# T in runs spread by ScalarE, the next Gram turn among the last rows, three edits in the last four chunks

## The chip, the cores and the metric

One core of a Trainium2 chip runs the whole program. The metric is the device time of one execution in microseconds (us). The kernel before was timed three times: 463.32, 463.43 and 470.28 us, median 463.43 us.

## The reference

Two blocks follow each other. The first is a delta-rule attention over 4 batches, 8 heads, 768 steps and head dimension 48; the second sends each of the 3072 tokens through one of 8 experts, chosen by a hash of its id.

```python
k_n = k / (np.linalg.norm(k, axis=-1, keepdims=True) + 1e-06)
for t in range(S):
    y[:, :, t] = einsum('bhd,bhde->bhe', q[:, :, t], state)
    v_old = einsum('bhde,bhd->bhe', state, k_n[:, :, t])
    state = state + beta_t * einsum('bhd,bhe->bhde', k_n[:, :, t], v[:, :, t] - v_old)
# x = y as (3072, 384)
for e in range(8):
    xe = x[expert == e]
    out[expert == e] = relu(xe @ w1[e]) @ w2[e]      # w1 384 x 1024, w2 1024 x 384
```

## The kernel before, in words

**Chunks and groups.** The 768 steps are cut into 24 chunks of 32 steps, and four chunks make a group, so there are six groups, 0 to 5. All batches and heads run together: 4 batches by 32 steps fill the 128 partitions. Within a chunk the recurrence is solved with the inverse T of a unit triangular matrix of 32 by 32 for each head and batch.

**The inverse (`inverse(g)`, VectorE).** For the four chunks of group g at once, a transpose of 32x32 blocks turns the Gram matrices (copied out of PSUM by ScalarE, L505) into NT, so that each partition holds one matrix (L628, "the Gram turn"). Then the norms follow: ssq (L630), a square root on ScalarE (root, L633), a short chain of small VectorE instructions (L635 to L649), and Ni (L652). Then 31 rows, each of a product (tmp, L664), a row (U, L660) and an addition (U, L668), each needing the one before. At the end one transpose takes U back to TU (L682), written with steps: one column of each block stands 32 elements from the next.

**The spread (`spread_t(g)`).** The matmul that applies T reads Tz, in which T stands twice, each time with half of the partitions set to zero. For group 0 and for the chunks 1 to 3 of each group this is done by four DMAs from TU (L592), issued by GpSimd and for the last group by SyncE; for the first chunk of groups 1 to 5 by two VectorE products with the columns of kmask (L584).

**A chunk (`chunk(c)`).** TensorE asks the state with the keys (L701 into bank A, on top of V scaled by VectorE in `scale_v`, L605); ScalarE copies the result to R (L733); TensorE asks with the queries into bank Y (L701); it multiplies R with Tz ("the T product", L743 bank<-R,Tz or solo<-R,Tz); ScalarE copies to W (L764); TensorE makes the Gram matrix of chunk c+9 (L485, while there is one) and the update of the state (L774); ScalarE copies the new state to S (L853), in the last four chunks VectorE copies half (L851); TensorE finishes the output with W and MT (L743 bank<-W,MT) and turns K and Q of chunk c+10 (L451). ScalarE copies the output to x_sb (L799), the turned keys to KQ (L461) and two masked copies to MT (L574); VectorE masks the Gram matrix of q and k (GQ, L508). GpSimd scatters x_sb to x_scratch in DRAM (`store`, L805). From chunk SOLO = 15 there is no Gram matrix left to make, and `scale_v`, the first ask, R, the T product and W go in two halves of four heads, the second half in a bank of its own (`home_a`).

**What sets the order.** Every step is a `task` with an engine, a duration that its author gave it, names that it reads and writes, and a boost. `order()` plays these tasks in time and picks on each engine the ready task with the longest rest; the instructions are then emitted in that order, so on every engine the order is fixed when the program is built, and an instruction that has to wait holds up all behind it on its engine.

**After the chunks.** `seven_first` (L112) multiplies the first 288 rows of expert 0 with w1; `turned` (L1472) then with w2. The first w1 and w2 are loaded in seven parts by GpSimd (`first_parts`, L180 and L183; the profile calls both homes w_first), after the stores of the chunks that PARTS lists. The other experts follow, bound to the same core.

Of the kernel before, what the change touches and what calls it, by code (L numbers as in the profile page):

```python
# [13 lines left out]
ACT = mybir.ActivationFunctionType  # L14
ALU = mybir.AluOpType
# [5 lines left out]
def kernel(  # L21
# [24 lines left out]
    QN = P // TB  # L46
# [141 lines left out]
    SP = mybir.EngineType.SP  # L188
# [12 lines left out]
    with ExitStack() as phase1:  # L201
        NU = S // C
        GC = 4
        NG = NU // GC
# [2 lines left out]
        L = C // 2  # L207
        NX = GC * H
        LEAD, AHEAD = 9, 10
        SPLIT, SOLO = NU - GC, NU - LEAD  # L210

        st = phase1.enter_context(tc.tile_pool(name="st", bufs=1))
# [5 lines left out]
        def quarter(b):  # L218
            return slice(C * b, C * b + C)
# [21 lines left out]
        TUs = tiles(2, "TU", [P, NX, C])  # L241
# [23 lines left out]
        kmask = st.tile([P, 2], F32)  # L265
# [15 lines left out]
        def task(eng, ns, reads, writes, emit, kb=0, kind=None, more=0, boost=0, apart=False,  # L281
                 size=0, shy=0):
            writes = tuple(writes) + tuple(x for w in writes for x in cleared.pop(w, ()))
            deps = {writer[r] for r in reads if r in writer}
            for r in reads:
                if r in BANKS and not apart:
                    deps |= {j for j in readers.get(r, ()) if tasks[j]["eng"] != eng}
            for w in writes:
                deps |= readers.get(w, set())
                if w in writer:  # L290
                    deps.add(writer[w])
            i = len(tasks)
# [12 lines left out]
            for w in writes:  # L305
                writer[w] = i
                readers[w] = set()
            return i
# [93 lines left out]
        def four(name):  # L402
            return tuple(f"{name}{b}" for b in range(B))
# [62 lines left out]
        hheads = (range(0, HU), range(HU, H))  # L466
# [109 lines left out]

        def spread_t(g):
            Tz, TU = Tzs[g % 2], TUs[g % 2]
            near = 1
            for cc in range(near if g else 0):  # L580
                xs_ = slice(H * cc, H * cc + H)
                for e in range(2):
                    task("DVE", 270, (f"TU{g % 2}",), (f"Tz{g % 2}{cc}{e}", f"Tz{g % 2}{cc}{e}+"),
                         lambda e=e, xs_=xs_: nc.vector.tensor_scalar(  # L584
                             out=Tz[:, xs_, e], in0=TU[:, xs_], scalar1=kmask[:, e:e + 1],
                             scalar2=None, op0=ALU.mult), boost=5e4)
            for b in range(B if near < GC else 0):
                x0 = H * near
                last = g == NG - 1
                task("SP" if last else "POOL", 450 if last else 800, (f"TU{g % 2}",),  # L590
                     [f"Tz{g % 2}{cc}{b % 2}" + "+" * (b // 2) for cc in range(near, GC)],
                     lambda b=b, x0=x0, eng=nc.sync if last else nc.gpsimd: eng.dma_start(  # L592
                         out=Tz[quarter(b), x0:, b % 2], in_=TU[quarter(b), x0:]),
                     kb=40 if last else 150)

        def scale_v(c):
            g = c // GC
            n = n_toks[g % 3][:, H * (c % GC):H * (c % GC) + H]
            if c == SOLO:
                late["solo"] = len(tasks) + 1  # L600
            for i, hs in enumerate(hheads if c >= SOLO else (range(H),)):
                m = len(hs)
                task("DVE", 482 if c < SOLO else 300, four(f"v{c % 4}_") + (f"ntok{g % 3}",),
                     ("A",) if i == 0 else ("P0", "P1", "P") if c == SOLO else ("P1",),
                     lambda i=i, hs=hs, m=m: nc.vector.tensor_tensor(  # L605
                         home_a(i)[:, 0:m * D].rearrange("p (h d) -> p h d", h=m),
                         Vs[c % 4][:, hs.start:hs.stop],
                         n[:, hs.start:hs.stop, None].to_broadcast([P, m, D]), op=ALU.mult),
                     shy=700 if c else 0)
# [4 lines left out]
        def inverse(g):  # L614
            i = g % 2
            U, Ni, n_tok = Us[i], Nis[i], n_toks[g % 3]
            ssq, root, rn, nd = [smalls[n][i] for n in ("ssq", "root", "rn", "nd")]

            def dve(ns, reads, writes, emit):
# [4 lines left out]
                U, zero[:, :, None].to_broadcast([P, C, C]), ACT.Copy), shy=24000 if g == 1 else 8000 if g else 0, boost=-6e4 if g else 0)  # L624
            task("DVE", 1165, tuple(f"GK{g % 3}{cc}{r}{b}" for cc in range(GC) for r in range(2)
                                     for b in (range(B) if g == 0 and cc < 2 else ("",))) + (
                f"U{1 - i}r{C - 1}",),
                 ("NT",), lambda: nc.vector.transpose(  # L628
                     NT, GKs[g % 3].rearrange("p j c u r -> p j (c u r)")))
            task("DVE", 100, ("NT",), (f"ssq{i}",), lambda: nc.vector.tensor_scalar(  # L630
                out=ssq, in0=NT.rearrange("p j i -> p (j i)")[:, ::C + 1], scalar1=1e-30,
                scalar2=None, op0=ALU.max))
# [4 lines left out]
                out=rn, in0=rn, scalar=0.25, in1=ssq, op0=ALU.mult, op1=ALU.mult))  # L637
            dve(105, ("root", "rn"), ("root",), lambda: nc.vector.scalar_tensor_tensor(
                out=root, in0=rn, scalar=1e-6, in1=root, op0=ALU.add, op1=ALU.add))
# [5 lines left out]
                     out=nd, in0=rn, scalar=-1.0, in1=beta_i[:, g], op0=ALU.mult, op1=ALU.mult))  # L645
# [24 lines left out]
            for j in range(C - 1):  # L670
                n, row = j + 1, f"Ni{i}_{0 if j < L else L}"
                rows = [f"U{i}r{x}" for x in range(C)]
# [6 lines left out]
                if n < C - 1:  # L679
                    task("DVE", ns, (f"U{i}", f"tmp{2 * i + j % 2}"), rows[n + 1:],  # L680
                         lambda j=j: ahead(j, "add"), kind="inv0" if g == 0 else "inv")
            task("DVE", 1810, (f"U{i}", *rows), (f"TU{g % 2}",), lambda: nc.vector.transpose(  # L682
                TUs[g % 2].rearrange("p x i -> p i x"), U))
            last_iv[0] = len(tasks) - 1

        last_iv, first = [0], {}
# [5 lines left out]

        def ask(c, a, bank, name):
            S0, KQ = Ss[c % 2], KQs[c % NKQ]
            apart = c >= SOLO and a == 0

            def go(us):
                res = home_a(us.start) if apart else bank
                x0 = us.start if apart else 0
                for u, b in pairs(us):  # L700
                    nc.tensor.matmul(res[quarter(b), 2 * D * (u - x0):2 * D * (u - x0 + 1)],  # L701
                                     lhsT=KQ[:, u, a, quarter(b)],
                                     rhs=S0[:, b, u].rearrange("p r d -> p (r d)"),
                                     start=(a == 1 and u == 0), stop=True,
                                     skip_group_check=True, tile_position=(0, C * b))

            for us in halves:
                task("PE", 345, held(c, a) + (f"S{c % 2}0", f"S{c % 2}1"),
                     ("P1",) if apart and us.start else (name,),
                     lambda us=us: go(us), kind="A", size=32)  # L710

        def chunk(c):
            g, cc = divmod(c, GC)
            R, W, x_sb = Rs[c % 2], Ws[c % 2], Xs[c % 2]
            TU, Tz, MT = TUs[g % 2], Tzs[g % 2], MTs[c % 2]
            x0 = H * cc
            flat_a, flat_y = bank_a[:, 0:H * D], bank_y[:, 0:H * D]
            turned, grams = next(to_turn, None), next(to_gram, None)
            busy = grams is not None
# [7 lines left out]

            if c > 0:
                ask(c, 0, bank_a, "A")
            for i, hs in enumerate((range(H),) if busy else hheads):  # L730
                task("ACT", 425 if busy else 300, ("P1" if i else "A",),
                     [f"R{c % 2}{x}" for x in range(2) if hheads[x].start in hs],
                     lambda i=i, hs=hs: nc.scalar.activation(  # L733
                         R[:, hs.start:hs.stop].rearrange("p h d -> p (h d)"),
                         home_a(i)[:, 0:D * len(hs)], ACT.Copy))
# [25 lines left out]
            for i, hs in enumerate((range(H),) if busy else hheads):  # L761
# [4 lines left out]
                         scale=-1.0))  # L766
            if busy:
                gram(grams, home="P")()
            if c < NU - 1:
# [14 lines left out]
                for r in range(2):  # L784
# [3 lines left out]
                         apart=True)  # L788
# [8 lines left out]
            if busy and grams % GC == GC - 1:  # L797
                inverse(grams // GC)
            task("ACT", 387, ("Y",), (f"x{c % 2}",), lambda: nc.scalar.activation(  # L799
                x_sb[:, :, 0:DQ].rearrange("p q (i r) -> p q i r", i=CO),  # L800
                flat_y.rearrange("p (q r i) -> p q i r", q=QN, i=CO), ACT.Copy, scale=-1.0))

            def store():
                nc.gpsimd.tensor_copy(x_sb[:, :, DQ], number[:, c])
# [30 lines left out]
                    task("POOL", 900, reads, names, lambda n=n: w_parts(regs[3], first.get(  # L835
                        "w2"))[n](nc.gpsimd), kb=512 if n < CO else 384)

        PARTS = (13, 14, 16, 19, 20, 21, 21)
        to_load = {w: iter(range(AHEAD + 1, NU)) for w in "kq"}
        to_turn, to_gram = iter(range(AHEAD, NU)), iter(range(LEAD, NU))  # L840

# [353 lines left out]
        with tc.manual_schedule():  # L1195
# [13 lines left out]
            for i, bits in enumerate((C - 1, C)):  # L1209
                nc.vector.tensor_scalar(out=low_i[:, i:i + 1], in0=row_i, scalar1=bits,  # L1210
                                        scalar2=None, op0=ALU.bitwise_and)
# [42 lines left out]
    with tc.tile_pool(name="w_pool2", bufs=2) as w_pool2, \  # L1254
# [248 lines left out]
        with tc.manual_schedule():  # L1503
# [25 lines left out]
            hs = {0: m_h.tile([P, FO, CAP], F32, name="h_sb")}  # L1529
# [35 lines left out]
            e = E - 2  # L1565
# [73 lines left out]
```

## Time and profile before

| what | before |
|---|---|
| median of three runs | 463.43 us |
| the profiled execution | 466.5 us |
| its span on the core | 464.9 us |
| TensorE busy | 424.5 us, 91% |
| VectorE busy | 372.6 us, 80% |
| ScalarE busy | 206.6 us, 44% |
| GpSimd busy | 180.2 us, 39% |
| mean granted TensorE clock | 0.957 |

The profile is of one execution. Its times are counted from the start of its span. A row of the view in order of time gives start, duration, engine, line, operation, the tile written and the tiles read, and in brackets the idle time of the engine before it with what ended it. Neighbouring instructions of one kind are merged into a row with their count. The duration of a short instruction overlaps with the next one's start, so what an instruction costs its engine is the distance to the next start.

### The profile page before, as it was taken

How to read it: one execution, taken by the hardware profiler on the slowest of the kernel's cores; microseconds unless marked ns; L12 is line 12 of the kernel's file. 1: busy time of each engine (PE TensorE's matmuls, PEld its weight loads, DVE VectorE, ACT ScalarE, POOL GpSimd, SP SyncE). 2: the span in 40 equal slices, each digit the busy share in tenths (PEclk: the TensorE clock that was granted, in tenths of full speed). 3: DMA queues.
4: the chain of work that ended last, by engine and by line, in shares of the span. 5: the costliest groups of instructions: out<-in, count | busy, mean ns of one | idle time of the engine just before them, and what ended most of it. 6: DMA issues, size and time to landing. Idle time of an engine off the chain costs nothing. (4 is left out here: it accounts for less than half of the span.)

```text
span 464.9 us, 17367 instructions
## 1 busy us (share of the span) xinstructions
PE 424.5 (91%) x7032; PEld 385.9 (83%) x7032; DVE 372.6 (80%) x1229; ACT 206.6 (44%) x477; POOL 180.2 (39%) x228
## 2 busy tenths in 40 slices
PE   6878888988987988789999999999999999999994
PEld 3765777877876877678999998998999999999983
DVE  6799899999899899988638888676977878746750
ACT  3568967776766677645342322031131221300220
POOL 9490412314113234224006250075371653707762
PEclk8588899999898899989999999999999999999998
DMA  7984645657557167344199990190651924101101
GB/s 139 136 158 104 111 96 110 126 107 131 98 109 123 42 147 188 94 89 131 64 256 327 327 312 30 43 310 28 178 192 19 287 76 146 38 5 33 34 31 49
DMA packets 100625, 58.38 MB, mean 126 GB/s; under 512 B 87254, under 2 KB 94945, under 8 KB 99648
## 3 DMA queue, kind: packets, MB, share of 16 engines
q1 hardware_dynamic: 91440, 40.06, 37.0%
q0 software_dynamic: 7824, 16.87, 13.2%
q8 instruction: 56, 0.92, 0.9%
q10 hardware_dynamic: 1280, 0.32, 0.4%
q14 instruction: 25, 0.20, 0.2%
HBM read 44.51 MB, written 10.65 MB: 119 GB/s over the span
## 5 line engine op out<-in xcount | busy, mean ns | idle before, releaser
L1480 POOL DMA_INDIRECT out_dram<-o_sb,idx x81 | 87.5, 1080 | 104.0 <-DVE part L101 59.0
L805 POOL DMA_INDIRECT x_scratch<-x_sb,slot x24 | 25.6, 1066 | 108.2 <-ACT x_sb L799 35.1
L664 DVE TENSOR_TENSOR tmp<-U,Ni 128x30 f32<-128x30 f32 (+9 forms) x180 | 57.9, 322 | 0.1
L668 DVE TENSOR_TENSOR U<-U,tmp 128x30 f32<-128x30 f32 (+9 forms) x180 | 57.9, 322 | 0.0
L701 PE MATMUL bank<-S,KQ 128*32 128x96 f32 x1328 | 36.6, 258 | 6.4 <-ACT S L853 5.4
L660 DVE SCALAR_TENSOR_TENSOR U<-U,Ni 128x1 f32<-128x1 f32 (+30 forms) x186 | 42.2, 227 | 0.3
L853 ACT ACTIVATE S<-psS 48x768 f32<-48x768 f32 x43 | 34.6, 805 | 17.3 <-PE psS L774 16.8
L701 PEld LDWEIGHTS bank<-S,KQ 128*32 128x32 f32 x1328 | 30.0, 115 | 11.0 <-ACT S L853 8.1
L112 PE MATMUL first<-xT,w_sb 128*128 128x190 f32 (+3 forms) x150 | 32.8, 327 | 0.0
L774 PE MATMUL psS<-W,K 32*112 32x96 f32 x736 | 27.3, 276 | 4.4 <-issue 3.1
L743 PE MATMUL bank<-W,MT 64*64 64x48 f32 x768 | 29.5, 226 | 1.8 <-issue 1.7
L164 ACT ACTIVATE h_sb<-h_sb 128x392 f32<-128x392 f32 (+3 forms) x28 | 14.7, 525 | 36.2 <-DVE h_sb L101 36.2
L101 DVE TENSOR_TENSOR h_sb<-part,first 128x196 f32<-128x196 f32 (+3 forms) x63 | 20.3, 352 | 12.5 <-PE first L112 11.7
L743 PEld LDWEIGHTS bank<-W,MT 64*64 64x64 f32 x768 | 26.1, 140 | 4.6 <-issue 2.4
L774 PEld LDWEIGHTS psS<-W,K 32*112 32x112 f32 x736 | 22.6, 177 | 7.7 <-issue 3.8
L112 PE MATMUL first<-h_sb,w_sb 128*128 128x380 f32 (+4 forms) x96 | 27.7, 442 | 0.0
L101 DVE TENSOR_TENSOR part<-part,first 128x196 f32<-128x196 f32 (+4 forms) x50 | 17.5, 349 | 11.9 <-PE first L112 5.0
L112 PEld LDWEIGHTS first<-xT,w_sb 128*128 128x128 f32 x150 | 25.9, 190 | 0.0
L416 POOL DMA_DIRECT2D Q<-in_q_dram x40 | 23.1, 585 | 6.9 <-PE early L451 6.6
L112 PEld LDWEIGHTS first<-h_sb,w_sb 128*128 128x128 f32 x96 | 21.8, 254 | 4.8
L592 POOL DMA_DIRECT2D Tz<-TU x20 | 14.6, 738 | 26.6 <-ACT R L733 12.4
L112 PE MATMUL first<-x_sum,w_sum 128*128 128x196 f32 (+3 forms) x126 | 24.0, 326 | 0.0
(292 smaller groups left out, 1031.4 us busy)
## 6 DMA issues: line engine op xcount, KB each, us to landing
w_sb<-in_moe_w_dram SPq DMA_DIRECT2D x10, 1536.0 KB
w_first<-in_moe_w_dram SPq DMA_DIRECT2D x4, 1536.0 KB
V<-in_v_dram SPq DMA_DIRECT2D x96, 48.0 KB
K<-in_k_dram SPq DMA_DIRECT2D x89, 48.0 KB
Q<-in_q_dram SPq DMA_DIRECT2D x56, 48.0 KB
xr<-x_scratch SPq DMA_DIRECT2D x16, 145.5 KB
Q<-in_q_dram POOLq DMA_DIRECT2D x40, 48.0 KB, 3.7
Tz<-TU POOLq DMA_DIRECT2D x20, 96.0 KB
```

What stands on the lines that cost most here:

```text
L101: return lambda: nc.vector.tensor_tensor(out, a, b, op=ALU.add)
L112: nc.tensor.matmul(out, lhsT=lhsT, rhs=rhs, start=start, stop=True, skip_group_check=True)
L416: eng].dma_start(out=dst[quarter(b)],
L660: nc.vector.scalar_tensor_tensor(out=U[:, n, 0:n], in0=U[:, j, 0:n], scalar=Ni[:, j, n:n + 1], in1=U[:, n, 0:n], op0=ALU.mult, op1=ALU.add)
L664: nc.vector.tensor_tensor(t, U[:, j:n, 0:n].to_broadcast([P, m, n]), Ni[:, j, n + 1:, None].to_broadcast([P, m, n]), op=ALU.mult)
L668: nc.vector.tensor_tensor(U[:, n + 1:, 0:n], U[:, n + 1:, 0:n], t, op=ALU.add)
L701: nc.tensor.matmul(res[quarter(b), 2 * D * (u - x0):2 * D * (u - x0 + 1)], lhsT=KQ[:, u, a, quarter(b)], rhs=S0[:, b, u].rearrange("p r d ...
L743: nc.tensor.matmul(to[rows, h - h0], lhsT=lhsT(rows, h), rhs=rhs[rows, h], start=(first and h == h0), stop=True, skip_group_check=True, ti ...
L774: nc.tensor.matmul(late["S"][0:DP + D, b, 2 * D * u:2 * D * u + 2 * D], lhsT=K4[quarter(b), u].rearrange("p r d -> p (r d)")[:, 0:DP + D], ...
L805: put = nc.gpsimd.indirect_dma_start(out=x_dram[:, :], out_offset=bass.IndirectOffsetOnAxis(ap=slot[:, c:c + 1], axis=0), in_=x_sb.rearran ...
L853: put = nc.scalar.activation(S1[half(r), :, :, r], new[half(r), :, :, r], ACT.Copy)
L1480: scat = nc.gpsimd.indirect_dma_start(out=out_q, out_offset=bass.IndirectOffsetOnAxis(ap=of[:, k:k + 1], axis=0), in_=o_sb[:, k], in_offse ...
```

## The change

Four things are changed.

- The Gram turn (NT) of a group waited in the plan for the last row (31) of the inverse before; it now waits for row 26. The norms hang on it.
- For groups 1 to 5 the transpose of U writes TU in one run (step inside, head and chunk innermost), and the spread reads it in that order. All eight spreads of a group (four chunks, two halves) are now ScalarE instructions with kmask as scale; only for group 5 the first one is VectorE's. The 20 DMAs of groups 1 to 5 are gone. Group 0 stays as it was.
- In the last four chunks: chunk 20 (SPLIT) is no longer split in halves up to R; the copy to x_sb gets a boost in chunks 19 to 22; and the four parts of w2 are asked for after chunks 22, 22, 23, 23 and no longer after 19, 20, 21, 21.
- The durations in the plan go with it (TU 1150 for 1810, a spread 440 on ScalarE, 330 on VectorE).

```diff
-            for cc in range(near if g else 0):
+            by_i = TU.rearrange("p x i -> p (x i)").rearrange("p (i x) -> p i x", x=NX)
+            for cc in range(GC):
                 xs_ = slice(H * cc, H * cc + H)
                 for e in range(2):
-                    task("DVE", 270, (f"TU{g % 2}",), ...
+                    out = Tz[:, xs_, e].rearrange("p x i -> p i x")
+                    if cc == 0 and e == 0 and g in SHARED:        # SHARED = (NG - 1,)
+                        task("DVE", 330, (f"TU{g % 2}",), names, ... tensor_scalar(
+                                 out=out, in0=by_i[:, :, xs_], scalar1=kmask[:, 0:1], ...), boost=5e4)
+                    else:
+                        task("ACT", 440, (f"TU{g % 2}",), names, ... activation(
+                                 out, by_i[:, :, xs_], ACT.Copy, scale=kmask[:, e:e + 1]),
+                             boost=0 if cc else 4e4)
-            for b in range(B if near < GC else 0):
-                task("SP" if last else "POOL", ... dma_start(
-                         out=Tz[quarter(b), x0:, b % 2], in_=TU[quarter(b), x0:]), ...)
...
+        def solo(c):
+            return c >= SOLO and c != SPLIT
...
-                f"U{1 - i}r{C - 1}",),
+                f"U{1 - i}r{C - 6}",),
                  ("NT",), lambda: nc.vector.transpose(
...
-            task("DVE", 1810, (f"U{i}", *rows), (f"TU{g % 2}",), lambda: nc.vector.transpose(
-                TUs[g % 2].rearrange("p x i -> p i x"), U))
+            task("DVE", 1150 if g else 1810, (f"U{i}", *rows), (f"TU{g % 2}",),
+                 lambda: nc.vector.transpose(
+                     TUs[g % 2].rearrange("p x i -> p (x i)").rearrange("p (i x) -> p i x", x=NX)
+                     if g else TUs[0].rearrange("p x i -> p i x"), U))
...
-                flat_y.rearrange("p (q r i) -> p q i r", q=QN, i=CO), ACT.Copy, scale=-1.0))
+                flat_y.rearrange("p (q r i) -> p q i r", q=QN, i=CO), ACT.Copy, scale=-1.0),
+                 boost=4e4 if SPLIT - 1 <= c < NU - 1 else 0)
...
-        PARTS = (13, 14, 16, 19, 20, 21, 21)
+        PARTS = (13, 14, 16, 22, 22, 23, 23)
```

## Rows read from the trace of the kernel before

**Rows 1.** The page's first part: busy time, share of the span and instructions.

```profile
PE 424.5 (91%) x7032; PEld 385.9 (83%) x7032; DVE 372.6 (80%) x1229; ACT 206.6 (44%) x477; POOL 180.2 (39%) x228
```

**Rows 2.** Busy time by stretch: three periods of an inverse, then the experts.

```profile
core 0: us, PE busy (x) PEld busy (x) DVE busy (x) ACT busy (x) POOL busy (x), PEclk, DMA share, GB/s
77.90:106.40 28.50, 24.87 (x887) 21.61 (x882) 27.94 (x112) 20.66 (x39) 7.64 (x11) 1.00 0.59 118
...
137.20:169.40 32.20, 28.84 (x929) 25.61 (x924) 30.16 (x117) 22.14 (x42) 8.88 (x13) 0.89 0.51 103
169.40:196.50 27.10, 22.02 (x712) 19.32 (x708) 26.80 (x116) 18.39 (x41) 9.67 (x15) 1.00 0.60 139
...
240.00:465.00 225.00, 218.04 (x1227) 207.16 (x1225) 161.01 (x379) 47.33 (x140) 100.60 (x96) 0.99 0.45 134
```

**Rows 3.** By line: duration in ns, least, median, most, of the two transposes.

```profile
L628 DVE STREAM_TRANSPOSE NT<-w_first x6: 1209/1239/1245, 17.6 to 168.2; 128x1024 f32<-128x1024 f32 x6
...
L682 DVE STREAM_TRANSPOSE TU<-U x6: 1911/1960/2016, 44.7 to 196.5; 128x1024 f32<-128x1024 f32 x6
```

**Rows 4.** In order of time, VectorE: spread and Gram turn, then the last TU.

```profile
79.98 0.62 DVE L584 TENSOR_SCALAR Tz<-TU,kmask 128x256 f32<-128x256 f32 x2
80.51 1.24 DVE L628 STREAM_TRANSPOSE NT<-w_first 128x1024 f32<-128x1024 f32 x1
...
196.46 1.95 DVE L682 STREAM_TRANSPOSE TU<-U 128x1024 f32<-128x1024 f32 x1
```

**Rows 5.** Waits, 46 to 200 us: total us, times, longest.

```profile
DVE rn L635 <- ACT root L633: 2.2, 4, 1.4
...
ACT root L633 <- DVE ssq L630: 6.6, 4, 2.0
...
PE pair L451 <- DVE GQ L508: 2.8, 3, 1.1
...
PE bank L743 <- DVE Tz L584: 1.5, 1, 1.5
```

**Rows 6.** ScalarE by shape, 46 to 222 us: count, busy us, mean ns, idle before.

```profile
L574 ACT ACTIVATE MT<-GQ,kmask 128x256 f32<-128x256 f32 x48 | 22.8, 507 | 0.2 <-PE bank L743 0.2
...
L505 ACT ACTIVATE w_first<-pair 128x256 f32<-128x256 f32 x15 | 9.3, 618 | 3.3 <-PE pair L485 3.2
...
L764 ACT ACTIVATE W<-bank 128x384 f32<-128x384 f32 x15 | 7.3, 490 | 7.3 <-PE bank L743 7.3
L764 ACT ACTIVATE W<-solo 128x192 f32<-128x192 f32 x18 | 6.0, 331 | 8.6 <-PE solo L743 7.7
```

**Rows 7.** In order of time, TensorE: asks and T products around chunks 12, 16, 20.

```profile
143.19 1.53 PE L701 MATMUL bank<-S,KQ 128*32 128x96 f32 x64 [0.76 <-ACT S L853]
...
173.15 0.54 PE L701 MATMUL bank<-S,KQ 128*32 128x96 f32 x16 [1.22 <-ACT S L853]
...
196.58 0.54 PE L701 MATMUL bank<-S,KQ 128*32 128x96 f32 x16 [0.75 <-ACT S L853]
198.72 0.54 PE L701 MATMUL solo<-S,KQ 128*32 128x96 f32 x16 [1.60 <-DVE solo L605]
...
200.34 1.95 PE L743 MATMUL solo<-R,Tz 64*64 64x48 f32 x32
...
206.33 0.87 PE L701 MATMUL bank<-S,KQ 128*32 128x96 f32 x32 [0.82 <-ACT x_sb L799]
207.12 1.14 PE L743 MATMUL solo<-R,Tz 64*64 64x48 f32 x32
...
212.12 1.13 PE L743 MATMUL solo<-R,Tz 64*64 64x48 f32 x32
```

**Rows 8.** The last store, the product with w2, and the DMAs of w2.

```profile
221.09 1.11 POOL L805 DMA_INDIRECT x_scratch<-x_sb,slot  x1 [1.26 <-ACT K L149]
...
230.58 11.85 PE L1472 MATMUL first<-h_first,w_first 128*128 128x288 f32 x48
...
w_first<-in_moe_w_dram POOLq DMA_DIRECT2D x4, 384.0 KB, 3.7
```

More of the change, by code (lines that the diff above doesn't have):

```diff
@@ L209 @@
         LEAD, AHEAD = 9, 10
+        SHARED = (NG - 1,)
         SPLIT, SOLO = NU - GC, NU - LEAD
@@ L578, in spread_t @@
             Tz, TU = Tzs[g % 2], TUs[g % 2]
-            near = 1
-            for cc in range(near if g else 0):
+            if g == 0:
+                for b in range(B):
+                    task("POOL", 800, ("TU0",),
+                         [f"Tz0{cc}{b % 2}" + "+" * (b // 2) for cc in range(1, GC)],
+                         lambda b=b: nc.gpsimd.dma_start(
+                             out=Tz[quarter(b), H:, b % 2], in_=TU[quarter(b), H:]), kb=150)
+                return
+            by_i = TU.rearrange("p x i -> p (x i)").rearrange("p (i x) -> p i x", x=NX)
@@ L581, in spread_t @@
+            for cc in range(GC):
                 xs_ = slice(H * cc, H * cc + H)
                 for e in range(2):
[L583 to L586, printed above, removed]
-            for b in range(B if near < GC else 0):
[L588 to L594, printed above, removed]
+                    out = Tz[:, xs_, e].rearrange("p x i -> p i x")
+                    names = (f"Tz{g % 2}{cc}{e}", f"Tz{g % 2}{cc}{e}+")
+                    if cc == 0 and e == 0 and g in SHARED:
+                        task("DVE", 330, (f"TU{g % 2}",), names,
+                             lambda xs_=xs_, out=out: nc.vector.tensor_scalar(
+                                 out=out, in0=by_i[:, :, xs_], scalar1=kmask[:, 0:1],
+                                 scalar2=None, op0=ALU.mult), boost=5e4)
+                    else:
+                        task("ACT", 440, (f"TU{g % 2}",), names,
+                             lambda e=e, xs_=xs_, out=out: nc.scalar.activation(
+                                 out, by_i[:, :, xs_], ACT.Copy, scale=kmask[:, e:e + 1]),
+                             boost=0 if cc else 4e4)
@@ L600, in scale_v @@
                 late["solo"] = len(tasks) + 1
-            for i, hs in enumerate(hheads if c >= SOLO else (range(H),)):
+            for i, hs in enumerate(hheads if solo(c) else (range(H),)):
                 m = len(hs)
-                task("DVE", 482 if c < SOLO else 300, four(f"v{c % 4}_") + (f"ntok{g % 3}",),
+                task("DVE", 300 if solo(c) else 482, four(f"v{c % 4}_") + (f"ntok{g % 3}",),
                      ("A",) if i == 0 else ("P0", "P1", "P") if c == SOLO else ("P1",),
@@ L694, in ask @@
             S0, KQ = Ss[c % 2], KQs[c % NKQ]
-            apart = c >= SOLO and a == 0
+            apart = solo(c) and a == 0
             def go(us):
@@ L729, in chunk @@
                 ask(c, 0, bank_a, "A")
-            for i, hs in enumerate((range(H),) if busy else hheads):
-                task("ACT", 425 if busy else 300, ("P1" if i else "A",),
+            for i, hs in enumerate(hheads if solo(c) else (range(H),)):
+                task("ACT", 300 if solo(c) else 425, ("P1" if i else "A",),
                      [f"R{c % 2}{x}" for x in range(2) if hheads[x].start in hs],
```

## The prediction

> **What bounds the kernel now.** I read the page's first part, then the busy time by stretch, then the waits, then the order of time around the ends of the inverses. The first part names TensorE as busiest [rows 1], but that is a mean over two stages. In the stretch from 240 us on, the experts, TensorE is busy 218.04 of 225 us [rows 2]: that stage simply follows whatever comes before, and every microsecond saved earlier reaches the end. So the question is when chunk 23 ends.
>
> In the three periods of an inverse VectorE is busy 27.94 of 28.5, 30.16 of 32.2 and 26.80 of 27.1 us [rows 2]: it nearly never stops, and group 5's inverse cannot end before it has gone through all of this. TensorE is busy 22 to 29 us of the same periods and ScalarE 18 to 22. That makes VectorE the first bound. But a second one runs close beside it. The chain of chunks (ask, R, T product, W, update, S, next ask) meets VectorE's results only at the end of a group, and the first ask of chunk 20 starts at 196.58 us, when the copy of the state before it is done, while the last TU starts at 196.46 us [rows 4, 7]. The two bounds arrive together, so what is taken from VectorE alone counts only as far as the chunks also come sooner. This decides my sum.
>
> **VectorE's own saving, up to the start of the last TU.** (a) The transpose that writes in one run exists already: NT, same 128x1024 shape, 1.24 us, against 1.96 us for TU [rows 3]. I take 0.72 us for each of the four TUs of groups 1 to 4: 2.9 us. The lower bound is zero, were the step not the reason; both are the same instruction on the same shape, so I take the whole. (b) The two spreads cost VectorE the distance from 79.98 to 80.51 us, 0.53 us [rows 4]; four groups: 2.1 us. (c) VectorE waits for the root four times, 2.2 us in all [rows 5]; with the Gram turn started after row 26, ssq and root run while rows 27 to 31 are worked on, so I take all 2.2 us. Interleaving may close further small gaps between dependent instructions; I count nothing for these. Together 7.2 us.
>
> Against that, a Gram turn among the rows puts its 1.24 us and the norms ahead of the TU of the group before. VectorE's total is unchanged by it, but the first T product of each group waits for that TU. The 1.46 us that TensorE now waits there once [rows 5] can return at each of the four boundaries.
>
> **The chunks' saving, up to chunk 20.** Three kinds of waits hang on the work that is changed. TensorE waits 1.5 us for Tz once and 2.8 us in three waits for GQ on VectorE [rows 5]; I take two of the three to stand behind TU and Tz, 1.9 us. ScalarE stands idle for ssq four times, 6.6 us [rows 5], with the copy of the state queued behind the root; TensorE shows this as 0.76 us before chunk 12's ask and 1.22 us before chunk 16's [rows 7], 2.0 us. Together 5.4 us if all go.
>
> Then what ScalarE gets. Groups 1 to 4 add 32 spreads before chunk 20, none of which existed there. **The price of one** is in no row. The lower bound is MT: same shape, same kmask scale, 0.507 us [rows 6]. The new one writes in steps, as L505 does, which takes 0.618 us for 256 elements; W takes 0.490 for 384 and 0.331 for 192 elements, 0.83 ns for an element, so 256 in one run would be 0.384 us, and the step adds 0.234 us [rows 6]. Upper bound: 0.507 + 0.234 = 0.74 us. I take the upper one, since L505 is the row with the same kind of write. Neighbours overlap by about 0.10 us, as elsewhere on this engine, so 0.64 us of the engine each (0.40 at the lower bound), 20.5 us for 32.
>
> What hides them: ScalarE's idle 7.8, 10.1 and 8.7 us in the three periods [rows 2], against 5.1 us for a group's eight. The idle is in pieces: before W it is 7.3 us over 15 copies, about half a microsecond each, and before L505 0.2 us [rows 6]. An op of 0.64 us doesn't quite fit into such a piece. I charge the chain a fifth, 0.13 us an op, 4.1 us for 32. The ends of that: nothing, and the whole 20.5 us. What is left to the chunks is 5.4 - 4.1 = 1.3 us.
>
> Here stands one rule against the change. The VectorE spread costs its engine 0.27 us and a ScalarE one at least 0.40 [rows 4, 6], so the work grows while it moves. The Trainium skill says as much (ScalarE: Activation LUTs, Rules for kernel authors): multiplications belong on VectorE. The trace agrees on the price of one, not that it decides. By that rule the first two spreads would stay on VectorE, at 0.53 us a group.
>
> **Chunk 20.** Its second ask now waits 1.60 us for the second half of scaled V, queued behind TU on VectorE [rows 7]. In one piece, that product stands ahead of TU. Both asks in one go take 1.53 us at full clock (the one at 143.19 [rows 7]); with 0.3 us more for R the T product could start at 198.4 in place of 200.34 us: 1.9 us. It needs its Tz by then: a TU of 1.24 and two spreads side by side on two engines, 0.74 us, ends 2.0 us after TU's start, so TU must start 0.1 us sooner relative to the chunks. VectorE's 7.2 us against the chunks' 1.3 gives that amply.
>
> **Chunks 20 to 23.** From T product to T product it takes 6.78 us after chunk 20 and 5.00 after chunk 21 [rows 7]. Of the 1.78 us more, 0.82 are the wait for x_sb, which the boost addresses, and 0.8 the T product itself, 1.95 in place of 1.14 us, after TensorE's idle 1.60. I take 1.3 us of it.
>
> **Edits at nothing.** The 16 DMAs of GpSimd and 4 of SyncE that go were needed by chunks a period later; the stores queued behind on GpSimd wait for ScalarE anyway. The fetch of expert 0's rows into TU0 waits for group 4's last spread instead of its last DMA; that spread is due by chunk 19's T product, and if it runs only then, the fetch and VectorE's work on these rows slip behind chunk 20, where VectorE has room. The w2 parts move behind the stores of chunks 22 and 23, which stay ahead of them in GpSimd's queue. The last store ends at 222.2 us; two to four issues of under 0.8 us each end by 225.4, and 3.7 us to landing gives 229.1, before 230.58, when TensorE wants w2 [rows 8]. The cover is 1.5 us at its thinnest; without it TensorE waits by what it lacks.
>
> **The sum.** 1.3 + 1.9 + 1.3 = 4.5 us off the profiled execution's 466.5 us, 462.0. That execution stands 3.1 us above the median of the runs shown, 463.43, so the median becomes **458.9 us**.
>
> **Rivals.**
> - *The chunks follow VectorE wholly.* If the spreads do fit into ScalarE's idle time and TensorE's clock no longer falls (0.89 granted in 137.2 to 169.4, 1.00 in its neighbours [rows 2]), VectorE alone decides: 7.2 us, then 1.8 from TU's start to the T product (3.9 now, 2.1 then), and 1.3: 10.3 us, 453.1. For it: VectorE's shares. Against it: the three engines would all be above nine tenths. Chance 0.14.
> - *ScalarE becomes the bound* (slower). The plan books a spread at 440 ns; at 0.64 us taken and put ahead of the R, W or S that everyone waits for, each delays the chain. The point from which it decides is (5.4 + 1.9 + 1.3) / 32 = 0.27 us an op. An op in the 0.2 us before L505 costs about 0.4, the most is 0.64; at 0.5 it is 16.0 - 8.6 = 7.4 us more, 470.8, and 475.3 at the most. For it: written in steps, and eight come due at once at each TU. Against it: six of eight have a chunk or more of time. Chance 0.16, a quarter of it above 472.7. The SBUF page of the Trainium skill (SBUF — State Buffer, Door 1) holds that each access to a new 16-byte line pays a penalty. The transposes agree, 1.24 against 1.96 us [rows 3]: by that rule the step isn't removed but carried from one transpose to eight spreads, and I have raised this chance for it.
> - *The Gram turn stays where it was.* The plan may still hold it behind the rows. Then the root's 2.0 us for the chunks stay, 4.5 becomes 2.5: 460.9. Chance 0.12.
>
> **How the numbers follow.** Forecast 0.58, between 455.5 and 462.5 by the bounds of a spread and the waits; the rivals 0.14, 0.16, 0.12. The range 452.0 to 466.5 takes in the first rival and the edge of the second and leaves out about 0.17. Two per cent, 9.3 us, is about what a measurement of this kernel can tell from no change: faster than 454.2 us has 0.12, most of the first rival; slower than 472.7 has 0.04; the rest, 0.84, is within.
>
> **What would show it.** TU of groups 1 to 5 near 1.24 us; a ScalarE spread at 0.50 to 0.74; no wait of rn for root and little of root for ssq; the L628 rows before the L682 of the group before; chunk 20's T product within 2.2 us of TU's start and at a full clock; 5.0 to 5.5 us to the next; no idle TensorE before L1472. The forecast is wrong if W, R or S wait behind spreads (slower), or if the wait of S for TensorE and of TensorE for S shrink with VectorE still busy throughout (faster).

## The result and the profile after

The changed kernel took 467.67 us (median of 12 runs) against 463.84 us for the kernel before, run beside it: a ratio of 1.0106, 95% interval 1.0081 to 1.0131. It is slower by one per cent; 458.9 was forecast. Ratios, here and below, compare the executions of the faster of two states in which this program runs, so they differ a little from the ratio of the medians (here 1.0083). The profiled execution lasts 466.98 us, its span 465.4 us. That is nearly the time of the profile before, whose execution lay 3 us above its median, so the two totals hide the loss. I compare from chunk 0's T product to the first product of expert 0 (L112): 46.86 to 219.63 us before, 172.8 us; 44.25 to 219.84 us after, 175.6 us. The chunks take 2.8 us more. TensorE's clock does not explain this pair: from 57 us to the experts it is at the lower level for 13.7 us before and for 10.2 us after.

The page's first part, after:

```profile
PE 421.2 (91%) x7032; PEld 383.2 (82%) x7032; DVE 365.4 (79%) x1219; ACT 224.0 (48%) x515; POOL 168.5 (36%) x212
```

Against [rows 1] VectorE is busy 7.2 us less and ScalarE 17.4 us more. By stretch, again from one TU to the next for three periods, then the experts:

```profile
core 0: us, PE busy (x) PEld busy (x) DVE busy (x) ACT busy (x) POOL busy (x), PEclk, DMA share, GB/s
78.65:106.40 27.75, 23.14 (x708) 20.62 (x710) 26.09 (x111) 21.54 (x42) 3.74 (x6) 0.88 0.47 97
132.21:162.00 29.79, 25.20 (x864) 21.88 (x863) 27.62 (x113) 25.21 (x48) 5.85 (x9) 1.00 0.39 83
162.00:194.05 32.05, 25.65 (x884) 22.90 (x886) 27.20 (x116) 24.95 (x56) 7.07 (x10) 1.00 0.47 118
240.00:465.00 225.00, 218.38 (x1227) 207.24 (x1225) 160.84 (x379) 47.21 (x140) 101.85 (x96) 0.99 0.46 135
```

The experts are as in [rows 2]. But VectorE now stands still for 1.7, 2.2 and 4.9 us of these periods, where it stood for 0.6, 2.0 and 0.3 us [rows 2]. Much of what it no longer does, it waits. The two transposes, by line (least, median, most in ns), and the spread on ScalarE (busy us, mean ns, idle before):

```profile
L640 DVE STREAM_TRANSPOSE NT<-w_first x6: 1216/1233/1245, 15.0 to 166.5; 128x1024 f32<-128x1024 f32 x6
```

```profile
L695 DVE STREAM_TRANSPOSE TU<-U x6: 1186/1245/1942, 42.2 to 194.0; 128x1024 f32<-128x1024 f32 x6
```

```profile
L600 ACT ACTIVATE Tz<-TU,kmask 128x256 f32<-128x256 f32 x39 | 24.4, 721 | 5.5 <-DVE TU L695 5.5
```

TU in a run costs 1.25 us in place of 1.96 [rows 3], and a spread 0.72 us, close to the 0.74 taken from [rows 6]. The last column is new: ScalarE stands 5.5 us waiting for TU with a spread at the head of its queue. The waits from 46 to 200 us, as in [rows 5]:

```profile
DVE GQ L509 <- ACT w_first L506: 6.0, 6, 2.1
PE psS L788 <- ACT W L778: 6.0, 8, 2.2
ACT Tz L600 <- DVE TU L695: 5.5, 5, 1.6
PE bank L715 <- ACT S L868: 5.1, 6, 1.7
...
PE bank L757 <- ACT Tz L600: 3.2, 1, 3.2
PE pair L452 <- DVE GQ L509: 3.2, 4, 1.1
...
ACT root L645 <- DVE ssq L642: 1.0, 1, 1.0
```

ScalarE's wait for ssq has gone from 6.6 to 1.0 us, as forecast. In its place TensorE's update waits 6.0 us for W, and VectorE waits 6.0 us for ScalarE's copy of the Gram matrix before GQ. From 46 to 222 us both are still 6.0 us; in the kernel before they were, in that stretch,

```profile
DVE GQ L508 <- ACT w_first L505: 1.5, 2, 1.3
...
PE psS L774 <- ACT W L764: 1.1, 1, 1.1
```

In order of time, VectorE, ScalarE and TensorE at the start of group 2's period, where chunk 4's T product needs TU and its spreads:

```profile
78.65 1.19 DVE L695 STREAM_TRANSPOSE TU<-U 128x1024 f32<-128x1024 f32 x1
...
79.87 2.78 ACT L600 ACTIVATE Tz<-TU,kmask 128x256 f32<-128x256 f32 x5 [0.59 <-DVE TU L695]
...
81.18 1.13 PE L757 MATMUL bank<-R,Tz 64*64 64x48 f32 x32 [3.22 <-ACT Tz L600]
...
82.42 0.55 ACT L778 ACTIVATE W<-bank 128x384 f32<-128x384 f32 x1
```

TensorE stands 3.22 us; before, the same place read

```profile
80.74 1.13 PE L743 MATMUL bank<-R,Tz 64*64 64x48 f32 x32 [1.46 <-DVE Tz L584]
```

Group 2's Gram turn and norms ran ahead of this TU (NT at 73.78 us; before, NT followed TU, [rows 4]), so that TU starts 34.4 us after chunk 0's T product where it started 31.0 us after it. Then two spreads in a row must be done on ScalarE. The Gram turn came ahead of TU at two of the four boundaries, this one and the next (NT at 102.46, TU at 106.40 us); at the other two it still followed (135.55 after 132.21, 166.5 after 162.00). The next rows show TU of group 4, which falls beside chunk 14's T product:

```profile
162.00 1.25 DVE L695 STREAM_TRANSPOSE TU<-U 128x1024 f32<-128x1024 f32 x1
162.02 1.28 PE L757 MATMUL bank<-R,Tz 64*64 64x48 f32 x32
...
163.28 1.25 ACT L600 ACTIVATE Tz<-TU,kmask 128x256 f32<-128x256 f32 x2 [1.30 <-DVE TU L695]
...
164.71 0.47 ACT L778 ACTIVATE W<-bank 128x384 f32<-128x384 f32 x1
...
165.23 1.04 PE L788 MATMUL psS<-W,K 32*112 32x96 f32 x32 [1.14 <-ACT W L778]
...
167.87 1.67 ACT L868 ACTIVATE S<-psS 48x768 f32<-48x768 f32 x2
...
169.59 0.54 PE L715 MATMUL bank<-S,KQ 128*32 128x96 f32 x16 [1.74 <-ACT S L868]
...
170.20 0.35 DVE L647 RECIPROCAL rn<-root 128x32 f32<-128x32 f32 x1 [2.17 <-ACT root L645]
```

The T product has ended at 163.3 us, but W waits behind two spreads until 164.71; the state's copy S waits behind four more, the ask behind S, and VectorE stands 2.17 us for a root that is queued behind S. From this T product to chunk 15's it takes 9.0 us (162.02 to 171.05); before, the same step took 6.3 (162.17 to 168.49). And at the last TU:

```profile
193.46 1.14 PE L757 MATMUL solo<-R,Tz 64*64 64x48 f32 x32
...
194.05 1.25 DVE L695 STREAM_TRANSPOSE TU<-U 128x1024 f32<-128x1024 f32 x1
195.32 1.23 ACT L600 ACTIVATE Tz<-TU,kmask 128x256 f32<-128x256 f32 x2 [1.63 <-DVE TU L695]
...
196.37 0.56 ACT L778 ACTIVATE W<-solo 128x192 f32<-128x192 f32 x2
...
196.77 1.04 PE L788 MATMUL psS<-W,K 32*112 32x96 f32 x32 [2.17 <-ACT W L778]
...
196.82 1.74 ACT L600 ACTIVATE Tz<-TU,kmask 128x256 f32<-128x256 f32 x3
...
198.37 0.84 ACT L868 ACTIVATE S<-psS 48x768 f32<-48x768 f32 x1
...
200.46 1.53 PE L715 MATMUL bank<-S,KQ 128*32 128x96 f32 x64 [1.58 <-ACT S L868]
...
202.54 1.13 PE L757 MATMUL solo<-R,Tz 64*64 64x48 f32 x32 [0.56 <-ACT R L747]
```

ScalarE has nothing but the spread in front from 193.7 us on, and waits for TU while W, whose product is ready at 194.6, stands behind. From chunk 19's T product to chunk 20's it is 9.1 us, before 7.8.

### The profile page after: what moved, and what is told of

It reads as the page before. It is cut to its first block, busy times and chain, and to the rows that moved or that the text cites. A ratio compares the mean times of both kernels' runs of the same rounds, so it can differ in the third digit from the quotient of the medians.

```text
span 465.4 us, 17345 instructions
## 1 busy us (share of the span) xinstructions
PE 421.2 (91%) x7032; PEld 383.2 (82%) x7032; DVE 365.4 (79%) x1219; ACT 224.0 (48%) x515; POOL 168.5 (36%) x212
## 5 line engine op out<-in xcount | busy, mean ns | idle before, releaser
L1495 POOL DMA_INDIRECT out_dram<-o_sb,idx x81 | 88.7, 1095 | 103.3 <-DVE part L101 59.0
L112 PE MATMUL first<-xT,w_sb 128*128 128x190 f32 (+3 forms) x150 | 32.8, 327 | 0.0
L757 PE MATMUL bank<-W,MT 64*64 64x48 f32 x768 | 30.5, 231 | 0.8 <-issue 0.8
L101 DVE TENSOR_TENSOR h_sb<-part,first 128x196 f32<-128x196 f32 (+3 forms) x63 | 20.2, 351 | 11.6 <-PE first L112 10.7
L112 PE MATMUL first<-h_sb,w_sb 128*128 128x380 f32 (+4 forms) x96 | 27.7, 442 | 0.0
L101 DVE TENSOR_TENSOR part<-part,first 128x196 f32<-128x196 f32 (+4 forms) x50 | 17.4, 349 | 12.3 <-PE first L112 5.5
L600 ACT ACTIVATE Tz<-TU,kmask 128x256 f32<-128x256 f32 x39 | 24.4, 721 | 5.5 <-DVE TU L695 5.5
L112 PEld LDWEIGHTS first<-xT,w_sb 128*128 128x128 f32 x150 | 25.9, 190 | 0.0
L112 PEld LDWEIGHTS first<-h_sb,w_sb 128*128 128x128 f32 x96 | 21.8, 254 | 4.8
L112 PE MATMUL first<-x_sum,w_sum 128*128 128x196 f32 (+3 forms) x126 | 24.0, 326 | 0.0
```

What stands on the lines that cost most here:

```text
L101: return lambda: nc.vector.tensor_tensor(out, a, b, op=ALU.add)
L112: nc.tensor.matmul(out, lhsT=lhsT, rhs=rhs, start=start, stop=True, skip_group_check=True)
L600: lambda e=e, xs_=xs_, out=out: nc.scalar.activation(out, by_i[:, :, xs_], ACT.Copy, scale=kmask[:, e:e + 1]),
L757: nc.tensor.matmul(to[rows, h - h0], lhsT=lhsT(rows, h), rhs=rhs[rows, h], start=(first and h == h0), stop=True, skip_group_check=True, ti ...
L1495: scat = nc.gpsimd.indirect_dma_start(out=out_q, out_offset=bass.IndirectOffsetOnAxis(ap=of[:, k:k + 1], axis=0), in_=o_sb[:, k], in_offse ...
```

## The experiments

Four series ran, each with the kernel before beside its kernels. In two of them the kernel before took 481 us, in the other two 465, so times are set side by side within a series only, and between series no more than ratios to the kernel before. The expectations give times on the scale of the first timing (463.8 us), so they too are read as ratios. "T product to experts" is the stretch measured above.

**Parts alone (kernel before: 480.98 us).** *only_spread*: the kernel before with the TU in runs and the spreads of the change, nothing else. *only_norms*: only the wait of NT, `r{C - 1}` to `r{C - 6}`. *only_tail*: only the edits of the last four chunks. *no_spread*: the changed kernel with TU, spread and DMAs as before.

> The kernel before with the spread alone: T in runs, the spread by ScalarE, nothing else. Theory 1 (ScalarE's queue): the spreads stand in ScalarE's queue ahead of W and S and wait there for TU, 5.5 us in the trace after, and this outweighs VectorE's 5.0 us; then this kernel alone is slower than before by at least as much as the whole change, 467 to 471 us, and the trace shows W or S copies behind spreads that wait for TU. Theory 2 (the Gram turn delays TU): the spread alone is a gain, 459 to 462 us.

> The kernel before with the Gram turn after row 26 alone. Theory 1: no loss, 460 to 464 us, since VectorE saves the 2.2 us that it waits for the root. Theory 2: the turn and the norms come ahead of TU, the first T product of each group waits 1.5 to 2.7 us longer at four boundaries, and the kernel is slower, 466 to 470 us.

> The kernel before with the three edits of the last four chunks alone. Both theories: a gain of 1 to 3 us, 461 to 463 us, from chunk 20's asks that no longer wait for the second half of scaled V and from the earlier x_sb; if the parts of w2 come too late, TensorE waits before the product with w2 and it is 1 to 3 us slower.

> The changed kernel with the spread undone (TU in columns, two VectorE products and four DMAs for a group); the Gram turn and the three edits of the last chunks stay. Theory 1: faster than before, 458 to 462 us. Theory 2: still slower than before, 465 to 469 us.

Measured: only_spread 1.0085 (1.0052 to 1.0118), only_norms 1.0060 (1.0016 to 1.0104), only_tail 0.9983 (0.9944 to 1.0022), no_spread 1.0085 (1.0045 to 1.0125). Both the spread and the early Gram turn lose by themselves, so neither needs the other to do harm; the edits of the last chunks, for which both theories wanted a gain of 1 to 3 us, can't be told from nothing. no_spread is the miss for theory 1, which wanted it faster than before: with no spread on ScalarE the early turn still loses. The losses don't add up: 0.85 and 0.6 alone, 1.06 together. Nor did only_spread show all of theory 1's picture: it loses 0.85% where at least the whole change's 1.06% was expected, and ScalarE waits 2.9 us for TU there, but the update only 1.3 us for W, near the 1.1 of the kernel before; what grew is VectorE's wait for the Gram copy, 5.1 us for 1.5.

**The Gram turn undone, then the spreads held, then the first ones back on VectorE (kernel before: 465.77 us).**

```diff
 turn_undone, against the changed kernel
-                f"U{1 - i}r{C - 6}",),
+                f"U{1 - i}r{C - 1}",),
 held_spreads, against turn_undone (shy: ns for which the plan prefers other ready work)
-                              boost=0 if cc else 4e4)
+                              boost=0 if cc else 4e4, shy=4000 if cc else 1500)
 first_on_vector, against held_spreads
-                    if cc == 0 and e == 0 and g in SHARED:
+                    if cc == 0:
                         task("DVE", 330, ... scalar1=kmask[:, e:e + 1], ...
```

> The changed kernel with the Gram turn waiting for row 31 again; the spread by ScalarE and the edits of the last chunks stay. The trace after has the turn and the norms ahead of TU in groups 1 and 2, and chunk 4's T product stands 37.0 us behind chunk 0's, 33.8 before. Theory 1 (two separate costs, the early turn at TU(1) and ScalarE's queue): chunk 4 comes back to 34 to 35.5 us behind chunk 0, and the kernel lands between before and the change, 1.002 to 1.008. Theory 2 (only the spread costs, the early turn is harmless beside it): no difference from the change, 1.009 to 1.013.

> As turn_undone, and in the plan the spreads become ready later (1.5 us for a group's first chunk, 4 us for the rest), so that W and S stand ahead of more of them in ScalarE's queue. Theory 1: the waits of the update for W and of the asks for S shrink, 0.998 to 1.004, below turn_undone. Theory 2 (it is ScalarE's load, 0.72 us a spread, not the place in the queue): the same as turn_undone within 0.003.

> As held_spreads, and both spreads of a group's first chunk are VectorE's again (reading T in runs), so that no T product at a boundary waits for ScalarE and no ScalarE instruction waits at its head for TU. Theory 1: the best of the three, 0.990 to 0.998, since TU's 0.7 us, the DMAs' absence and the last chunks' gain are left. Theory 2: ScalarE still has 30 spreads, 1.000 to 1.006.

Measured: turn_undone 1.0069 (1.0032 to 1.0106), held_spreads 1.0036 (0.9999 to 1.0073), first_on_vector 0.9900 (0.9867 to 0.9933), 460.97 us. The first two lie where theory 1 put them, the third at its lower edge. The wait of ScalarE for TU is not the price by itself: in turn_undone it is 7.3 us, more than in the changed kernel, while the update waits 2.6 us for W and the ratio is lower. held_spreads held the first chunk's spreads too, and chunk 4's T product waits 2.95 us for them; put on VectorE, that stand is 0.92 us, and the kernel is faster than both.

**One thing changed in first_on_vector (kernel before: 481.23 us).** *fov_turn*: the early Gram turn again. *fov_no_hold*: the spreads not held. *fov_columns*: TU in columns as before, so that ScalarE reads and writes runs. *fov_no_tail*: the last four chunks as before.

> first_on_vector (0.990) with the early Gram turn (row 26) put back. Theory 1 (the turn ahead of TU holds up the first chunk of a group whatever spreads T): slower than first_on_vector by 2 to 5 us, 0.994 to 1.001. Theory 2 (the early turn costs only beside the ScalarE queue): 0.988 to 0.992.

> first_on_vector without the hold: the 30 spreads of ScalarE are ready in the plan as soon as TU is. Theory 1 (place in the queue): slower than first_on_vector by 1 to 4 us, 0.992 to 0.999, with the update waiting for W behind spreads. Rival (only the first chunk's spreads matter, at the head of the queue): 0.988 to 0.992.

> first_on_vector with T in columns as before: TU 1.96 us again, and each ScalarE spread writes in runs, 0.50 us for 0.72. If T in runs is a gain by itself, VectorE loses 0.7 us a group and this is slower, 0.992 to 0.999; if the step that moves into the spreads costs ScalarE as much as VectorE gains, no difference, 0.988 to 0.992.

> first_on_vector without the three edits of the last four chunks. From chunk 20 on the trace after was 2.0 us quicker to the end than before, so 1 to 3 us slower than first_on_vector, 0.992 to 0.997; the rival, that the last chunks hang on VectorE's T alone, 0.988 to 0.991.

Measured: fov_turn 1.0054 (1.0014 to 1.0094), fov_no_hold 1.0046 (1.0002 to 1.0089), fov_columns 1.0009 (0.9967 to 1.0050), fov_no_tail 0.9969 (0.9924 to 1.0013). first_on_vector, against which the expectations were set, was not in this series. fov_turn and fov_no_hold came out slower than either of their theories said, fov_columns too; fov_no_tail lies at the edge of its first theory. Inside the series the variants with the early turn or without the hold are slower than the one without the last chunks' edits. In fov_columns the spread's mean falls to 508 ns, the price of MT [rows 6], while TU is back at 1.96 us; that is a price measured, not a gain in time.

**A ladder on one chip (kernel before: 464.67 us).** Each rung is one edit more: ladder_changed is the changed kernel; ladder_first takes the first chunk's spreads to VectorE; ladder_late_turn undoes the early Gram turn; ladder_hold holds the later spreads and is first_on_vector again.

> The changed kernel as it is, the lowest rung of a ladder of four, each one edit from the last, timed side by side. Every theory expects a ratio to the kernel before of 1.005 to 1.013, as in its first timing (1.011); if it comes out below 1.002 the loss itself depends on the chip and the three rungs above it cannot share it out.

> The changed kernel with one edit: in each group both spreads of the first chunk are VectorE's, where they were one of VectorE's and one of ScalarE's in the last group and both ScalarE's in the others. Theory A (ScalarE waits for the turn of U at the head of its queue, with W and S behind it, and that is what the chunks lose): the first spreads are those that wait, so ScalarE's waits for the turn of U fall from 5.5 us to under 3 us in 46 to 222 us and the ratio falls by 0.004 or more from the changed kernel's. Theory B (the early Gram turn loses the time by making the turn of U late): nothing gained, the ratio within 0.002 of the changed kernel's or above it, since VectorE only gets more to do. Theory C (VectorE is the bound): slower by 0.003.

> One more edit: the Gram turn waits again for the row just before the last one of the inverse, and not for the sixth from the end. Theory A: the Gram turn is worth 0.002 or less either way. Theory B: the ratio falls by 0.004 or more from the rung below, since the turn of U of the second group comes about 3 us earlier against the first chunk's T product. Theory C: no change of more than 0.002.

> One more edit, and with it the kernel that gave 0.990 in an earlier timing: the plan lets ScalarE's spreads of the later chunks wait up to 4 us for other work before they are put in the queue. Theory A: falls by 0.004 or more from the rung below, to 0.988 to 0.994, with ScalarE's waits for the turn of U near nothing. Theory B: within 0.003 of the rung below. If this kernel comes out above 0.997 here, its gain of one per cent on the other chip is not a property of the order alone, and each step's worth stays open.

| rung | median us | ratio (95%) | ScalarE waits for TU, us | update waits for W, us |
|---|---|---|---|---|
| ladder_changed | 470.69 | 1.0138 (1.0077 to 1.0199) | 5.6 | 6.0 |
| ladder_first | 467.27 | 1.0065 (1.0028 to 1.0102) | 2.3 | 3.2 |
| ladder_late_turn | 465.73 | 1.0042 (0.9999 to 1.0085) | 3.2 | 2.5 |
| ladder_hold | 461.68 | 0.9948 (0.9909 to 0.9987) | 0 | 1.3 |

The medians are over 12 executions, for ladder_changed over 6. The two wait columns are from 46 to 222 us of each profile. In this order the two rungs of theory A, ScalarE's queue, bring 3.4 and 4.0 us; the rung of theory B, the early turn, brings 1.5 us where B wanted 0.4% or more; theory C, VectorE as the bound, is unlikely, since the first rung gives VectorE more work and the median falls. The intervals of neighbours among the first three rungs overlap, so these steps are only probable; the last rung lies below the one before it, and the two ends are far apart. ladder_changed and ladder_hold lie just above the ranges expected for them (1.013 and 0.994 at most).

**The steps depend on each other.** fov_no_hold and ladder_late_turn are the same kernel, and fov_turn is ladder_first with the hold. So with the first spreads on VectorE all four combinations of the other two edits were measured (ratio to the kernel before in the same series):

| | spreads not held | spreads held |
|---|---|---|
| early Gram turn | 1.0065 (ladder_first) | 1.0054 (fov_turn) |
| late Gram turn | 1.0042 (ladder_late_turn), 1.0046 (fov_no_hold) | 0.9948 (ladder_hold), 0.9900 (first_on_vector) |

With the early turn the hold brings 0.1%, with the late turn 0.9% or more; undoing the early turn brings 0.2% without the hold and 1.1% or more with it. Only both together gain. So the 4.0 and 1.5 us of the rungs are not prices of these edits but of this order, and theory B is not out. The series differ by about 0.5% where they share a kernel (0.9948 and 0.9900), less than these differences.

ladder_hold around its last TU, in order of time:

```profile
188.90 1.13 PE L757 MATMUL solo<-R,Tz 64*64 64x48 f32 x32
...
189.68 0.80 ACT L778 ACTIVATE W<-solo 128x192 f32<-128x192 f32 x2 [0.54 <-PE solo L757]
...
190.06 1.11 PE L788 MATMUL psS<-W,K 32*112 32x96 f32 x32
...
191.34 1.25 DVE L695 STREAM_TRANSPOSE TU<-U 128x1024 f32<-128x1024 f32 x1
...
192.62 0.86 DVE L595 TENSOR_SCALAR Tz<-TU,kmask 128x256 f32<-128x256 f32 x2
...
193.71 1.53 PE L715 MATMUL bank<-S,KQ 128*32 128x96 f32 x64 [1.47 <-ACT S L868]
...
195.19 1.13 PE L757 MATMUL solo<-R,Tz 64*64 64x48 f32 x32
```

W follows the T product at once, and the next ask comes 4.8 us after it where the changed kernel needs 7.0. Chunk 20's T product comes 6.3 us after chunk 19's, not 9.1. From T product to experts it takes 166.9 us; before 172.8.

**What the clock adds.** The granted clock in 40 slices of the span (9 is full or nearly), ladder_changed first, ladder_hold second:

```profile
PEclk8589799797997999979999999999999999999999
```

```profile
PEclk8589599999999999999999999999999999999998
```

Both start low; after slice 5 the second never falls. Taken finer, the falls are stretches of 3.4 to 7 us, now and then longer, at the lower of the two levels (0.50, 1.2 GHz). The clearest case follows a stand of TensorE: in the seven profiles where chunk 4's T product had waited 2.56 to 3.22 us (after, only_norms, no_spread, held_spreads, fov_turn, ladder_changed, ladder_first), the clock falls as the wait ends or within 2.3 us, every time; in the other ten, where the longest stand of that place is 1.81 us, never. That chunk then takes 9.4 to 10.7 us to the next T product, in the other ten 6.6 to 7.8, so about 2.7 us on top of the wait. Elsewhere it is less clear: after shorter stands the clock sometimes falls and sometimes doesn't, before too (three times after the start in the profile shown), and in fov_turn it falls at 126.6 us with no stand over 1 us since chunk 4's. From 57 to 220 us the mean is 0.96 before, 0.97 after, 0.92 in ladder_changed, 1.00 in ladder_hold.

The mean granted clock is known for every timed execution, not for the profiled ones alone, and the time follows it: for the kernel before in the ladder's series 0.01 more goes with about 2.7 us less, over 29 executions from 0.931 to 0.981. An estimate from these: lines of one common slope through the executions of each kernel, read at a clock of 0.96, give 465.9 us for the kernel before and 468.5, 467.0, 465.9 and 463.4 for the rungs. Of the 9.0 us between the ends 5.1 are left at equal clock, and ladder_hold stays 2.5 us below the kernel before; first_on_vector stays 3.4 us below it (462.6 and 466.0). fov_turn, read the same way, lies 0.4 us below its kernel before (481.0 and 481.4), so a good part of what the early turn costs there goes with the clock. Whether the clock is the cause in this or an effect of the stands, these lines can't tell.

## Why the prediction was wrong

**The step that failed** is the charge for the spreads: "I charge the chain a fifth, 0.13 us an op, 4.1 us for 32." It took them for small pieces that fill ScalarE's idle time anywhere. The price of one was right (0.72 against 0.74 us), the place wasn't. A spread that the plan puts first is emitted first, and ScalarE then waits for TU with W, S and root behind it, things that TensorE and VectorE wait for. In the ladder's order the nine first spreads are worth 3.4 us, 0.38 us each, above the turning point of 0.27 that the second rival named; holding the 30 others is worth 4.0 us, 0.13 each, which equals the fifth by luck: with the early turn in place it is worth 0.1%. The mechanism of that rival, "put ahead of the R, W or S that everyone waits for", is what the rows after show. Its time, 470.8, is 7.4 us above the kernel before; measured were 3.8 us in the first timing and 6.0 in the ladder.

**The second step that failed has no price in the sum**: that TensorE's wait for Tz "can return at each of the four boundaries". It came back at chunk 4, 3.22 for 1.46 us, and with it a stretch at the lower clock. The prediction counted the early turn as a gain, 2.2 us of root on VectorE and 2.0 us of ssq for the chunks; alone it costs 0.6% (only_norms), with the last chunks' edits 0.85% (no_spread), and put back into first_on_vector it leaves 1.0054 where 0.9948 and 0.9900 were measured without it. So this step took the forecast gain away even without the first.

**VectorE's 7.2 us** came to the tenth, but by luck: 2.2 of the forecast 7.2 us were waits for the root, 5.0 were busy time up to the last TU. The 7.2 us measured are busy time over the whole execution, group 5's TU and spread included. Its waits for GQ's input grew by 4.5 us and for the root from 2.2 to 3.2, not to nothing: ssq comes earlier, yet root stands in the same queue behind S. Relative to chunk 0's T product VectorE is 4.7 us ahead at group 4's TU (117.8 against 122.5 us) and has lost it at group 5's (149.8 against 149.6). "The two bounds arrive together" was right; the chunks then went later, not sooner.

**The chunks' 5.4 us**: 3.4 of them were TensorE's waits for Tz and GQ, which are 3.2 and 3.2 us now, where they were 1.5 and 2.8. The other 2.0 were to come from asks that no longer wait for S behind the root; from 46 to 222 us the asks' waits for S are 6.7 us, where they were 5.4.

**Chunk 20 and after, 3.2 us.** Three parts did what was said: the second ask no longer waits, the T product runs at full clock in 1.13 us, and the next follows after 4.9 us. But chunk 20's T product came 8.5 us after TU's start, not 2.2, since the chunks were late. From chunk 19's T product to the experts it takes 26.4 us, before 27.1: 0.8 us arrived. only_tail shows 26.8 by the same count, and its time no difference.

**What held**: the edits at nothing. The w2 product starts at 230.72 us, before 230.58 [rows 8], and no DMA that went is missed. The rule of the Trainium skill that the prediction weighed (ScalarE: Activation LUTs, Rules for kernel authors) would have left the first two spreads on VectorE. The runs agree for these: ladder_first, 0.7% better. For the other six no run puts them on VectorE; held back on ScalarE with the late Gram turn, they cost no wait for TU, and first_on_vector beats the kernel before, which had them as DMAs.

**What stays open**: how much of first_on_vector's gain is VectorE's shorter work and how much the clock that no longer falls. Its two profiles show no stretch at the lower level after the start, the profile before three (117 to 121, 148 to 155, 199 to 203 us). At equal clock an estimated 3.4 and 2.5 us of its gain are left, but no run separates the clock from the stands. Why the hold gains only with the late turn was not traced. And the gain was 1.0% in one series and 0.5% in the other.

## What to carry to other kernels

Where an engine's order is fixed when the program is built, a small operation moved to a less busy engine is priced by what stands behind it while it waits for its input, not by the engine's idle share: ask whether its input is late, and hold it behind the work that others wait for. Here that paid only once the other late input, TU behind the early Gram turn, was put right too, so test edits together as well as one by one. Keep the one or two operations that the next step needs at once on the engine that made their input. And look at the longest stands of TensorE first: one of about 3 us was followed each time by a stretch at the lower clock that cost, by comparison of the profiles, nearly as much again.

## What the runs showed of the hardware

The same 128x256 spread takes ScalarE 0.51 us written in runs (fov_columns) and 0.72 us written in steps, and the transpose of 128x1024 takes VectorE 1.25 and 1.96 us: the step is paid wherever it is carried, 0.71 us once or 0.21 us eight times. (The spread written in steps also reads in runs of eight elements, so its 0.21 us may be partly the reading.) The SBUF page of the Trainium skill (SBUF — State Buffer, Door 1) says that each access to a new 16-byte line pays, and the trace agrees with it for both engines.

One and the same program took 3.5% longer (481 us for 465) in two of the series. The first series (480.98 us) and the ladder (464.67 us) ran under the same chip number, 8, so the chip alone is not the reason; what is stays open. In the profile of fov_columns, taken in the other series of 481 us, the experts start at 219.2 us, in the profile before at 219.6; the 15.7 us by which its span is longer (480.6 for 464.9) lie in the experts, not in the chunks that this change touches. There TensorE is busy 190.31 us from 260 to 460 us at a mean clock of 0.97; in the profile before 198.04 us at 1.00.
